# A fused attention and expert kernel: keys and queries transposed and copied one turn earlier, the queries' copy on ScalarE

## The chip, the core and the metric

The kernel runs on one core of a Trainium2 chip. The metric is the time of one execution on the device in microseconds (us). The work lies on five engines that run side by side, each through its own instructions in order: TensorE (PE; its weight loads are shown apart as PEld), VectorE (DVE), ScalarE (ACT), GpSimd (POOL) and SyncE (SP), which here issues the loads from memory.

## What is computed

Three layers in a row, all in 32-bit floats. The change lies in the first.

```python
# q, k, v: 2 batches x 8 heads x 768 positions x 64
k_sum = k.reshape(B, H, nb, 32, D).max(axis=3)      # one key per block of 32
v_sum = v.reshape(B, H, nb, 32, D).mean(axis=3)
scores_l = scale * q @ k.T        # kept where |row - column| < 16
scores_s = scale * q @ k_sum.T + log(32)
a = softmax(concatenate([masked scores_l, scores_s]))
x = a @ concatenate([v, v_sum])
# then: each of the 1536 rows of x goes through one of 8 experts (512 -> 1024 -> 512, relu),
# and all rows through w_in (512 -> 2048), h * cos(h), and w_out (2048 -> 512)
```

## The kernel before

**Pairs and turns.** Attention works on pairs of heads: 8 pairs (2 batches, 4 pairs of heads each), and each pair in two halves of 384 positions, so 16 halves. A loop of 18 turns (L1179) handles them as a pipeline. Half `h` belongs to pair `h // 2`. In turn `i` the engines do, in this order of the code:

- PE transposes the softmax weights of half `i-1` (`attn_turn`, L282, tile `pa`), computes the scores of half `i+1` (`attn_scores`, L247 and L256, tile `ps`) and, when `i` is even, the means of the values of a pair (`prep_v2`, L220, in the same `ps` tile);
- DVE adds the mask to the scores (L264) and takes the negated row maxima (L270, `nmx`); some turns also take the block maxima of the keys (`max_k`, L197, tile `ks`);
- ACT takes the exponentials of half `i` (L275), in even turns copies the values' means out of `ps` (L227, `vsm`), and copies the transposed weights out of `pa` (L290, `aT`);
- PE multiplies the weights of half `i-2` with the values (`attn_av`, L301, tile `po`) and DVE normalizes (L307, L308, L310) into `xb`, the layer's output.

**The keys and queries of a later pair.** They arrive from memory (`load_k`, `load_q`) with positions along the partitions. POOL puts the two heads side by side (`shuffle_k` and `shuffle_q`, L164, tiles `kr` and `qs`, one buffer each, so that a shuffle waits for the transposes that read the one before). PE transposes the result (`turn_heads`, L173) into the PSUM tile `pk` or `pq`, which share one buffer (tag `tr`), and an engine copies that to SBUF as `kT` (`prep_k`) or `qT` (`prep_q`): L186 when ACT does it, L188 when DVE does. There are two sets of `qT`, `kT` and `ks`; pair `n` uses set `n % 2`. At the end of turn `i` (L1242 to L1255) one of these steps is done: for the keys in odd turns, for the queries in even turns, of pair `(i+3)//2`. Pair `n`'s first scores are computed in turn `2n-1`, so its keys are prepared in turn `2n-3` and its queries in turn `2n-2`, the turn just before the scores. `maxima` sends `max_k` of the keys into the next turn (L1212). The names in `ON_VECTOR` (L54) say which copies DVE does; `q2 q4 q6 q8` are the queries' copies at the end of turns 2, 4, 6 and 8. The shuffle of the following pair and the load after that are issued right behind each step.

**What else stands in the turns.** `PLAN` (L47) places the routing to the experts of batch 0 into turns 8 to 13, and the scatter of its rows to memory (`route_scatter`, L536) into turn 13. The expert layer begins after turn 17, with the first 128 scattered rows read back (L745, `xw`), gated on POOL (L758), transposed (L772), copied to `xT` (L774, L775) and multiplied with the weights (L714, first tile `h`). The engines' order inside attention is that of the code (`manual_schedule`); a scheduler orders what follows.

Of the kernel before, what the change touches and what calls it, by code (L numbers as in the profile page):

```python
# [50 lines left out]
)  # L51


ON_VECTOR = "q2 q4 q6 q8 x2 x3 x5"  # L54
NWMAX = 24
TT = 384
TWO_PI = 2.0 * math.pi
# [48 lines left out]
def fused_kernel(ctx, tc, q, k, v, emb, tau, w1, w2, w_in, w_out, consts, out):  # L106
# [36 lines left out]
    def load_vw(b, g, half, vw):  # L143

        h0 = 2 * g
        t0 = 1 - half
        for hh in range(2):
            vs = v[b, h0 + hh]
            srcw = bass.AP(
                vs.tensor, vs.offset + (48 + 64 * (NU - 1) * half) * D,  # L150
                [[D, KW], [64 * D, NU - 1], [1, D]],
            )
            nc.sync.dma_start(vw[0:KW, hh, t0:t0 + NU - 1, 0:D], srcw)
        n = KW - WIN
        if half == 0:
            dst, src = vw[WIN:KW, :, 0, 0:D], v[b, h0:h0 + 2, 0:n]
        else:
            dst, src = vw[0:n, :, NU - 1, 0:D], v[b, h0:h0 + 2, S - n:S]
        nc.sync.dma_start(dst, src.rearrange("h c d -> c h d"))
# [36 lines left out]
    def max_k(bf):  # L196
        nc.vector.tensor_reduce(  # L197
            bf["ks"], bf["kT"][:, WIN:WIN + S].rearrange("d (n r) -> d n r", r=BLK),
            axis=AX.X, op=ALU.max,
        )  # L200
# [24 lines left out]
    def evac_v(pv, ap):  # L225
        vsm = ap.tile([P, 2, D], F32, tag="vsm", name="vsm", bufs=1)
        nc.scalar.activation(vsm[KW:KC], pv, AF.Copy)  # L227
        return vsm
# [8 lines left out]
    def attn_scores(half, bf, ps_s, ap, va=None):  # L237
        qT, kT, ks = bf["qT"], bf["kT"], bf["ks"]


        ps = ps_s.tile([P, 2, 512], F32, tag="s", name="ps")
        for u in range(NU // 2):
            for hh in range(2):
                for m in range(2):
                    t = NU * half + 2 * u + m
                    hp = slice(64 * hh, 64 * hh + 64)
                    nc.tensor.matmul(  # L247
                        ps[64 * m:64 * m + 64, hh, u * KC:u * KC + KW],
                        lhsT=qT[hp, t * 64:(t + 1) * 64], rhs=kT[hp, t * 64:t * 64 + KW],
                        start=True, stop=True,  # L250
                    )
        for u in range(NU // 2):
            for hh in range(2):
                t = NU * half + 2 * u
                hp = slice(64 * hh, 64 * hh + 64)
                nc.tensor.matmul(  # L256
                    ps[:, hh, u * KC + KW:(u + 1) * KC],
                    lhsT=qT[hp, t * 64:(t + 2) * 64], rhs=ks[hp, :], start=True, stop=True,
                )
        pv = ps[KW:KC, 0, 3 * KC:3 * KC + 2 * D].rearrange("p (h d) -> p h d", h=2)  # L260
        if va is not None:
            prep_v2(va, pv)
        s = ap.tile([P, NU, KC], F32, tag="s", name="s")
        nc.vector.tensor_tensor(  # L264
            s.rearrange("p (a u) c -> p a (u c)", a=2), ps[:, :, 0:3 * KC],
            mask[:, 3 * half * KC:3 * (half + 1) * KC].unsqueeze(1).to_broadcast([P, 2, 3 * KC]),
            op=ALU.add,
        )
        nmx = ap.tile([P, NU], F32, tag="nmx", name="nmx")
        nc.vector.tensor_reduce(nmx, s, axis=AX.X, op=ALU.max, negate=True)  # L270
        return s, nmx, pv

    def attn_exp(s, nmx):
        for u in range(NU):
            nc.scalar.activation(s[:, u, :], s[:, u, :], AF.Exp, bias=nmx[:, u:u + 1])  # L275

    on_vector = set(ON_VECTOR.split())

    def attn_turn(s, ps_a):
        pa = ps_a.tile([P, 8 * P], F32, tag="a", name="pa")[:, 0:NU * P]  # L280
        for u in range(NU):
            nc.tensor.transpose(pa[0:KC, u * P:(u + 1) * P], s[:, u, :], ident)  # L282
        return pa

    def attn_aT(pa, ap, i):
        aT = ap.tile([P, NU * P], F32, tag="aT", name="aT")
        if f"a{i}" in on_vector:
            nc.vector.tensor_copy(aT[0:KC], pa[0:KC])
        else:
            nc.scalar.activation(aT[0:KC], pa[0:KC], AF.Copy)  # L290
        return aT
# [694 lines left out]
    with ExitStack() as actx:  # L986
# [50 lines left out]
        NPR = len(pairs)  # L1037
# [16 lines left out]
        def shuffle_k(n):  # L1054

            if n < NPR:
                shuffle(kns[n % 2], krt, nc.gpsimd)
            if n + 2 < NPR:
                load_k(n + 2)
# [7 lines left out]
        def pair_v(n, eng):  # L1067
            if n < NPR:
                prep_v1(vns[n % 2], va, eng)
            if n + 2 < NPR:  # L1070
                load_v(n + 2)
# [95 lines left out]
        def at(i, place):  # L1167
            for piece in plan.get((i, place), ()):
                next(piece, None)
# [9 lines left out]
        for i in range(NH + 2):  # L1179
            p, odd = divmod(i, 2)  # L1180
            if i == 3:
                nc.sync.dma_start(cst[:, P:], consts[:, P:C_VIND])
                next(setup)
                for b, xb in enumerate(xbs):
                    nc.gpsimd.memset(xb[:, :, DM:ROW], 0.0)
                    nc.gpsimd.tensor_copy(
                        xb[:, :, DM:DM + 1],
                        csa[:, C_TOK - C_VIND + b * NU:C_TOK - C_VIND + (b + 1) * NU].unsqueeze(2),
                    )
            if i == 10:  # L1190
                zt = wp.tile([P, 1024], F32, tag="raw", name="zt", bufs=4)[:, 0:ROW]
                nc.gpsimd.memset(zt[:, 0:DM], 0.0)
                nc.gpsimd.memset(zt[:, DM:ROW], 1e6)
                for r0 in (S, NTOK):
                    nc.sync.dma_start(
                        xs[r0:r0 + WT].rearrange("(a p) d -> p a d", p=P),
                        zt.unsqueeze(1).to_broadcast([P, WT // P, ROW]),
                    )
            at(i, "0")
            if 0 < i <= NH:  # L1200
                pa = attn_turn(ss.pop(i - 1), ps_a)
            at(i, "p")
            pv = None
            if i + 1 < NH:
                n, half = divmod(i + 1, 2)
                sums = half and 0 < n < NPR - 1
                ss[i + 1], nmx[i + 1], pv = attn_scores(
                    half, sets[n % 2], ps_s, ap, va if sums else None
                )
                if not sums:  # L1210
                    pv = None
            if maxima is not None:  # L1212
                max_k(maxima)
                maxima = None
            at(i, "s")
            if i < NH:
                attn_exp(ss[i], nmx.pop(i))
            if pv is not None:
                vsm = evac_v(pv, ap)
                pair_v(n + 2, nc.gpsimd)  # L1220
            if 0 < i <= NH:
                aTs[i - 1] = attn_aT(pa, ap, i)
            at(i, "c")
            if i >= 2:
                b, g = pairs[p - 1]
                last_av = attn_av(g, odd, aTs.pop(i - 2), sets[(p - 1) % 2], xbs[b], ps_s, ap)
                if p + 1 < NPR:
                    load_vw(*pairs[p + 1], odd, sets[(p + 1) % 2]["vw"][odd])
                    if odd:
                        prep_v3(sets[(p + 1) % 2], vsm)  # L1230
            at(i, "h")
            if i < 2:
                prep_v3(sets[i], means_v(va))
                pair_v(i + 1, nc.gpsimd)
                load_vw(*pairs[1], i, sets[1]["vw"][i])
            if i == 0:
                prep_k(sets[1], kr, two_banks(), (nc.scalar, nc.vector))
                max_k(sets[1])
                shuffle_k(2)
                prep_q(sets[1], qs, ps_t, nc.scalar)  # L1240
                shuffle_q(2)
            n = (i + 3) // 2  # L1242
            if i and n < NPR:
                if odd:
                    pk = ps_t.tile([P, 8, P], F32, tag="tr", name="pk")
                    prep_k(
                        sets[n % 2], kr, [pk], [nc.vector if f"k{i}" in on_vector else nc.scalar]
                    )
                    maxima = sets[n % 2]
                    shuffle_k(n + 1)  # L1250
                else:
                    prep_q(
                        sets[n % 2], qs, ps_t, nc.vector if f"q{i}" in on_vector else nc.scalar
                    )
                    shuffle_q(n + 1)  # L1255
            at(i, "e")
# [205 lines left out]
```

## Time and profile before

| what | value |
|---|---|
| time, median of 3 runs | 569.94 us (567.6 to 570.23) |
| time of the profiled execution | 571.92 us |
| its span, first to last instruction | 569.9 us |
| mean granted clock of TensorE | 0.959 of full speed |
| PE busy | 526.1 us (92%) |
| DVE busy | 400.1 us (70%) |
| ACT busy | 299.8 us (53%) |
| POOL busy | 94.7 us (17%) |

The profile is of one execution. Its span leaves out what lies before the first and after the last instruction, 2.0 us here. A row of a timeline gives the start from the beginning of the span, the time taken, engine, line, operation, the tile written and the tiles read, shapes and how many instructions are merged; in brackets stands the idle time of the engine just before, and what ended it. The last of several things waited for is named, and at times it is named wrongly. Turn 3 begins on PE at 30.57 us, turn 4 at 35.95, turn 5 at 41.24, turn 7 at 53.48, and turn 9 at 67.35 (there with transposes for the routing).

### The profile page before, as it was taken

Reading aid. Unit: us, or ns where it says so; the run is one execution under the profiler, and the core shown is the slowest. Engines: PE = TensorE matmul, PEld = TensorE weight load, DVE = VectorE, ACT = ScalarE, POOL = GpSimd, SP = SyncE. Lnnn points to the kernel's source line nnn. Section 1 sums busy time; section 2 is a strip of 40 time slices with the busy share of each in tenths; the row PEclk is TensorE's granted clock in tenths of the full one; section 3 lists DMA queues with packets and bytes.
Section 4 is the critical chain, followed back from the end, with each engine's and each line's share of the span. In section 5 each row is a group of like instructions: output and inputs, shape, how many; then the busy total and the mean of one; then the engine's idle time right before and its main releaser. Section 6 shows DMA issues by size and latency. Waiting matters only on the chain. (4 is left out here: it accounts for less than half of the span.)

```text
span 569.9 us, 10621 instructions
## 1 busy us (share of the span) xinstructions
PE 526.1 (92%) x3968; PEld 480.4 (84%) x3968; DVE 400.1 (70%) x830; ACT 299.8 (53%) x637; POOL 94.7 (17%) x116
## 2 busy tenths in 40 slices
PE   6978886759998999999999999999999999999993
PEld 5866765647888999999999998999999999999992
DVE  2476558668677667798977999896579956556662
ACT  2665347758836566575655676643355433333330
POOL 2553323439145110000000000000000000002222
PEclk9798799759999999999999999999999999999998
DMA  8786322778569665767640433322001000001111
GB/s 242 213 229 161 93 96 63 237 275 272 181 212 301 198 217 174 234 200 245 197 136 1 148 114 116 105 74 75 0 1 39 1 1 0 1 0 56 56 57 59
DMA packets 49226, 72.37 MB, mean 127 GB/s; under 512 B 21256, under 2 KB 27656, under 8 KB 49168
## 3 DMA queue, kind: packets, MB, share of 16 engines
q1 hardware_dynamic: 46336, 62.13, 35.9%
q0 software_dynamic: 2832, 9.49, 4.5%
q8 instruction: 33, 0.54, 0.4%
q14 instruction: 25, 0.20, 0.1%
HBM read 64.24 MB, written 7.37 MB: 126 GB/s over the span
## 5 line engine op out<-in xcount | busy, mean ns | idle before, releaser
L714 PE MATMUL po<-sl,gt 128*128 128x512 f32 x567 | 139.3, 390 | 0.0
L714 PEld LDWEIGHTS po<-sl,gt 128*128 128x128 f32 x567 | 105.6, 188 | 17.7
L714 PE MATMUL ph<-yT,sl 128*128 128x384 f32 x576 | 109.6, 339 | 0.0
L714 PEld LDWEIGHTS ph<-yT,sl 128*128 128x128 f32 x576 | 102.8, 188 | 3.8
L624 DVE TENSOR_TENSOR sl<-raw,sl 128x512 fp32r<-128x512 f32 x112 | 73.4, 689 | 17.5 <-ACT sl L623 17.0
L623 ACT ACTIVATE sl<-raw 128x512 fp32r<-128x512 f32 x112 | 64.4, 625 | 22.4 <-PE py L714 12.9
L714 PE MATMUL py<-ht,sl 128*128 128x256 f32 x576 | 72.5, 282 | 0.2 <-DVE ht L810 0.2
L714 PE MATMUL ph<-xT,sl 128*128 128x256 f32 x576 | 71.7, 282 | 0.0
L714 PEld LDWEIGHTS ph<-xT,sl 128*128 128x128 f32 x576 | 69.6, 189 | 0.7 <-issue 0.6
L714 PEld LDWEIGHTS py<-ht,sl 128*128 128x128 f32 x576 | 68.9, 188 | 1.0 <-issue 0.6
L967 POOL DMA_INDIRECT out_dram<-acc,perm x12 | 12.0, 1000 | 344.8 <-DVE acc L1372 342.4
L924 ACT ACTIVATE u<-u 128x384 f32<-128x384 f32 x64 | 33.6, 524 | 62.5 <-DVE u L923 62.4
L928 ACT ACTIVATE gt<-t 128x384 fp32r<-128x384 f32 x63 | 33.1, 525 | 31.3 <-DVE t L927 31.1
L920 ACT ACTIVATE t<-ph 128x384 f32<-128x384 f32 x64 | 31.3, 489 | 33.4 <-PE ph L714 33.0
L927 DVE TENSOR_TENSOR t<-ph,u 128x384 f32<-128x384 f32 (+1 forms) x66 | 35.7, 544 | 17.7 <-ACT u L924 17.4
L929 DVE TENSOR_TENSOR gt<-t,gt 128x384 fp32r<-128x384 f32 x63 | 35.1, 556 | 17.2 <-ACT gt L928 17.2
L922 DVE TENSOR_SCALAR u<-t 128x384 f32<-128x384 f32 x64 | 22.9, 358 | 29.1 <-ACT t L920 27.4
L714 PE MATMUL ph<-yT,early 128*128 128x384 f32 x192 | 36.3, 338 | 0.2 <-DVE yT L1319 0.2
L923 DVE TENSOR_TENSOR u<-t,u 128x384 f32<-128x384 f32 x64 | 35.5, 555 | 1.1
L714 PEld LDWEIGHTS ph<-yT,early 128*128 128x128 f32 x192 | 34.0, 188 | 1.6 <-DVE yT L1319 0.5
L264 DVE TENSOR_TENSOR s<-ps,csa 128x720 f32<-128x720 f32 x16 | 14.5, 907 | 29.4 <-PE ps L256 16.1
L275 ACT ACTIVATE s<-s,nmx 128x120 f32<-128x120 f32 x96 | 29.0, 382 | 8.1 <-DVE nmx L270 6.7
(182 smaller groups left out, 674.2 us busy)
## 6 DMA issues: line engine op xcount, KB each, us to landing
raw<-in_moe_w_dram SPq DMA_DIRECT2D x56, 512.0 KB, 4.5
raw<-in_moe_w_in_dram SPq DMA_DIRECT2D x16, 512.0 KB, 3.7
raw<-in_moe_w_out_dram SPq DMA_DIRECT2D x16, 512.0 KB, 4.3
vw<-in_v_dram SPq DMA_DIRECT2D x32, 120.0 KB, 3.5
xw<-xs POOLq DMA_DIRECT2D x6, 516.0 KB
kn<-in_k_dram SPq DMA_DIRECT2D x8, 384.0 KB, 6.4
qr<-in_q_dram SPq DMA_DIRECT2D x8, 384.0 KB, 4.4
vn<-in_v_dram SPq DMA_DIRECT2D x8, 384.0 KB, 6.8
```

The costliest lines, as they stand in the source:

```text
L264: nc.vector.tensor_tensor(s.rearrange("p (a u) c -> p a (u c)", a=2), ps[:, :, 0:3 * KC], mask[:, 3 * half * KC:3 * (half + 1) * KC].unsqu ...
L275: nc.scalar.activation(s[:, u, :], s[:, u, :], AF.Exp, bias=nmx[:, u:u + 1])
L623: nc.scalar.activation(sl[:, 0, c], r, AF.Copy)
L624: nc.vector.tensor_tensor(sl[:, 1, c], r, sl[:, 0, c].bitcast(F32), op=ALU.subtract)
L714: nc.tensor.matmul(acc, lhsT=lw(a), rhs=lx(c), start=(first and i == 0), stop=(last and i == 2))
L920: nc.scalar.activation(t, ph, AF.Copy, scale=1.0 / TWO_PI, bias=0.25)
L922: nc.vector.tensor_scalar(u, t, ROUND, -ROUND, op0=ALU.add, op1=ALU.add)
L923: nc.vector.tensor_tensor(u, t, u, op=ALU.subtract)
L924: nc.scalar.activation(u, u, AF.Sin, scale=TURN)
L927: nc.vector.tensor_tensor(g, ph[:, cs], u[:, cs], op=ALU.mult)
L928: nc.scalar.activation(gt[:, 0], g, AF.Copy)
L929: lo = nc.vector.tensor_tensor(gt[:, 1], g, gt[:, 0].bitcast(F32), op=ALU.subtract)
```

## The change

The queries leave `ON_VECTOR`, so ACT makes all their copies. The pair that is prepared at the end of turn `i` is now `i // 2 + 2`: its keys in even turns, its queries in odd turns, from turn 0 on. So pair `n`'s keys are prepared in turn `2n-4` and its queries in turn `2n-3`, each one turn earlier than before, and the last step falls in turn 11 and no longer in turn 12.

```diff
-ON_VECTOR = "q2 q4 q6 q8 x2 x3 x5"
+ON_VECTOR = "x2 x3 x5"
...
-            n = (i + 3) // 2
-            if i and n < NPR:
-                if odd:
+            n = i // 2 + 2
+            if n < NPR:
+                if not odd:
                     pk = ps_t.tile([P, 8, P], F32, tag="tr", name="pk")
                     prep_k(
                         sets[n % 2], kr, [pk], [nc.vector if f"k{i}" in on_vector else nc.scalar]
```

The order of PE at the end of turn 0 and in turn 1 (`pk`, `pq`: transposed keys and queries; `pa`: weights; `ps`: scores; `pv`: means of the values), where the first unchanged row is the keys of pair 1:

```order
 L173 MATMUL pk<-cst,kr 128x128 x6
 L173 MATMUL pq<-cst,qs 128x128 x6
+L173 MATMUL pk<-cst,kr 128x128 x6
 L282 MATMUL pa<-cst,s 120x128 x6
 L247 MATMUL ps<-kT_135,qT_134 64x96 x12
 L256 MATMUL ps<-ks_136,qT_134 128x24 x6
 L220 MATMUL pv<-va,csa 24x128 x3
-L173 MATMUL pk<-cst,kr 128x128 x6
+L173 MATMUL pq<-cst,qs 128x128 x6
```

The keys of pair 2 now stand ahead of the first weights' transposes, and the queries of pair 2 take the place that these keys had; from there on keys and queries swap places turn by turn.

ACT from the exponentials of turn 3 to those of turn 5, before:

```order
L275 ACTIVATE s<-s,nmx 128x120 x6
L290 ACTIVATE aT<-pa 120x768
L186 ACTIVATE kT_135<-pk 128x768
L275 ACTIVATE s<-s,nmx 128x120 x6
L227 ACTIVATE vsm<-ps 24x128
L290 ACTIVATE aT<-pa 120x768
L348 ACTIVATE esq,en<-big 8x512
L275 ACTIVATE s<-s,nmx 128x120 x6
```

and with the change:

```order
L275 ACTIVATE s<-s,nmx 128x120 x6
L290 ACTIVATE aT<-pa 120x768
L186 ACTIVATE qT_134<-pq 128x768
L275 ACTIVATE s<-s,nmx 128x120 x6
L227 ACTIVATE vsm<-ps 24x128
L290 ACTIVATE aT<-pa 120x768
L186 ACTIVATE kT_130<-pk 128x768
L348 ACTIVATE esq,en<-big 8x512
L275 ACTIVATE s<-s,nmx 128x120 x6
```

The even turn has a keys' copy where ACT had none, between `aT` and the next exponentials; in the odd turn the copy is that of queries.

DVE at the end of turn 4, in turn 5 (second L264) and up to turn 5's normalizing (`tauc` is a routing constant):

```order
 L310 TENSOR_TENSOR xb_218<-po,rs 128x3x128
-L188 TENSOR_SCALAR qT_134<-pq 128x768
 L350 RECIPROCAL tauc<-tauc 128x1
 L264 TENSOR_TENSOR s<-ps,csa 128x720
 L270 TENSOR_REDUCE nmx<-s 128x6
+L197 TENSOR_REDUCE ks_131<-kT_130 128x24
 L307 TENSOR_SCALAR rs<-po 128x6
 L308 RECIPROCAL rs<-rs 128x6
```

The queries' copy is gone from DVE, and the block maxima of the keys have come from the even turn into the odd one.

## Rows read from the trace of the kernel before

**Rows 1.** Busy time by stretch: PE, PEld, DVE, ACT, POOL (instructions), granted clock, DMA share, GB/s.

```profile
30.57:41.24 10.67, 8.64 (x150) 7.32 (x151) 6.97 (x13) 6.00 (x17) 4.81 (x10) 1.00 0.88 204
41.24:53.48 12.24, 10.54 (x154) 8.97 (x154) 7.88 (x17) 6.60 (x19) 4.57 (x7) 0.86 0.63 174
53.48:67.35 13.87, 11.72 (x151) 10.07 (x151) 7.09 (x14) 5.95 (x16) 4.68 (x6) 0.75 0.39 103
...
126.15:569.90 443.75, 430.00 (x2650) 400.42 (x2650) 328.19 (x674) 233.40 (x470) 47.99 (x43) 0.99 0.35 113
```

**Rows 2.** PE's timeline, turns 0 to 5: start, us, what, idle before.

```profile
20.45 1.48 PE L282 MATMUL pa<-cst,s 128*120 128x128 f32 x6
...
27.44 0.84 PE L220 MATMUL ps<-va,csa 128*24 128x128 f32 x6 [0.42 <-POOL va L213]
...
30.57 0.87 PE L282 MATMUL pa<-cst,s 128*120 128x128 f32 x6 [0.58 <-ACT aT L290]
32.90 0.73 PE L247 MATMUL ps<-kT,qT 64*64 64x96 f32 x24 [1.46 <-DVE qT L188]
...
35.95 0.82 PE L282 MATMUL pa<-cst,s 128*120 128x128 f32 x6
...
41.24 0.87 PE L282 MATMUL pa<-cst,s 128*120 128x128 f32 x6 [0.56 <-ACT aT L290]
43.60 0.72 PE L247 MATMUL ps<-kT,qT 64*64 64x96 f32 x24 [1.48 <-DVE qT L188]
```

**Rows 3.** What PE waited for from 30.57 to 126.2: total us, times, longest.

```profile
PE ps L247 <- DVE qT L188: 4.5, 3, 1.6
...
PE pxa L368 <- DVE xb L310: 1.5, 2, 0.9
```

**Rows 4.** DVE's timeline in turn 4.

```profile
39.08 0.91 DVE L264 TENSOR_TENSOR s<-ps,csa 128x720 f32<-128x720 f32 x1 [1.81 <-PE ps L220]
...
40.84 0.94 DVE L197 TENSOR_REDUCE ks<-kT 128x24 f32<-128x768 f32 x1
...
42.59 0.95 DVE L188 TENSOR_SCALAR qT<-pq 128x768 f32<-128x768 f32 x1
```

**Rows 5.** ACT's timeline, turns 1 to 4.

```profile
24.25 0.27 ACT L227 ACTIVATE vsm<-pv 24x128 f32<-24x128 f32 x1 [0.34 <-PE pv L220]
...
36.15 0.81 ACT L186 ACTIVATE kT<-pk 128x768 f32<-128x768 f32 x1 [3.23 <-PE pk L173]
36.86 1.81 ACT L275 ACTIVATE s<-s,nmx 128x120 f32<-128x120 f32 x6
40.08 0.27 ACT L227 ACTIVATE vsm<-ps 24x128 f32<-24x128 f32 x1 [1.42 <-POOL va L213]
40.38 0.81 ACT L290 ACTIVATE aT<-pa 120x768 f32<-120x768 f32 x1
```

**Rows 6.** POOL's timeline, turns 0 and 3.

```profile
21.05 0.83 POOL L164 TENSOR_SCALAR kr<-kn 128x768 f32<-128x768 f32 x1
...
35.40 0.83 POOL L232 TENSOR_SCALAR vw<-vsm 24x768 f32<-24x768 f32 x1 [2.94 <-DMA vw<-in_v_dram]
```

**Rows 7.** PE's timeline, turns 10 to 13.

```profile
88.19 0.39 PE L437 MATMUL pr<-oh,cst 128*128 128x48 f32 x2 [2.91 <-DVE rs L307]
...
98.49 0.87 PE L282 MATMUL pa<-cst,s 128*120 128x128 f32 x6 [1.19 <-ACT aT L290]
101.10 1.24 PE L247 MATMUL ps<-kT,qT 64*64 64x96 f32 x24 [1.74 <-ACT qT L186]
```

**Rows 8.** DVE's timeline, turns 12 and 13.

```profile
101.18 0.17 DVE L476 TENSOR_SCALAR gate<-gate 128x6 f32<-128x6 f32 x1
103.79 0.91 DVE L264 TENSOR_TENSOR s<-ps,csa 128x720 f32<-128x720 f32 x1 [2.44 <-PE ps L256]
```

**Rows 9.** POOL's timeline: the first of six scatters, turn 13.

```profile
106.69 1.60 POOL L536 DMA_INDIRECT xs<-xb,posi  x1 [0.48 <-DVE big L310]
```

**Rows 10.** PE's timeline: the first matmuls of the expert layer.

```profile
126.15 1.22 PE L714 MATMUL h<-sl,xT 128*128 128x512 f32 x2 [2.92 <-DVE xT L775]
```

## The prediction, made before the changed kernel ran

> **What bounds the kernel now.** I read the busy time by stretch first. From 126.15 us on, the expert layers keep PE at work for 430.0 of 443.75 us at a clock of 0.99, so nothing is to be had there; attention before it has gaps [rows 1]. A pair of turns takes 10.67 us at full clock (30.57 to 41.24, PE busy 8.64), then 12.24 us at 0.86, then 13.87 us at 0.75. If attention ends earlier, the expert layer starts earlier, and PE-bound work behind it moves as a whole.
>
> PE's timeline and its waits show the gaps. In turns 3, 5 and 7 the scores wait for `qT` on DVE: 1.46 and 1.48 us in the rows, 4.5 us for three, so the third took 1.6 [rows 2, 3]. The weights' transposes ahead of them wait 0.58 and 0.56 us for `aT` on ACT [rows 2]. DVE's timeline says why `qT` is late: its copy stands last in a queue of work that begins with the mask at 39.08, has `max_k` at 40.84 (0.94 us), and comes to `qT` at 42.59, ending at 43.54; the scores start at 43.60 [rows 4, 2]. PE had finished the transposes long before.
>
> ACT's timeline shows the other chain. The copy of the means (`vsm`) starts at 40.08, right behind the mask's end at 39.08 + 0.91 = 39.99; the profile names POOL, but both read the same PSUM tile and I read it as a wait for the mask [rows 4, 5]. Then `aT` runs from 40.38 to 41.19, and turn 5 begins on PE at 41.24. This chain holds no query copy, so the change leaves it.
>
> **The change, part by part.** The sum is against the profiled execution, 571.92 us, which lies 2.0 us above the median of the three runs, 569.94; I carry the difference over to the median.
>
> 1. *The start, turns 0 to 2: a loss of 1.9 us.* In turn 0 the keys of pair 2 now go ahead of `pa`, which began at 20.45 [rows 2]. They need POOL's shuffle, which ends at 21.05 + 0.83 = 21.88 [rows 6]. With 0.7 us for the six transposes (turn 3's `pa` group of the same six matmuls, 0.87 with its drain, bounds it from above) `pa` begins at about 22.65, 2.2 us late. ACT has the keys' copy (0.81 us, the row of 36.15) ahead of the exponentials and of `vsm`; `vsm` had 0.34 us of waiting to give, so the lag there is 1.85 us [rows 5]. It goes on through POOL's `va`, for which PE already waited, to the means at 27.44 [rows 2]. Bounds: nothing lost, were the shuffle early, and 2.2 + 1.3 us if PE's clock, still low at 20.45 (1.48 us for six transposes against 0.82 at 35.95), rises later. I take 1.9, from the chain's own rows.
>
> 2. *Turns 3, 5 and 7: 1.46 + 1.48 + 1.6 = 4.5 us gained* [rows 2, 3]. The queries were copied a turn before, so scores start right behind `pa`. Turn 3's part pays back most of the start. What is late next is `aT` in even turns, the 0.56 us that stay; I expect a pair of turns at 10.67 - 1.48 = 9.2 us.
>
> 3. *The copies on ACT: nothing on the path.* DVE loses four of 0.95 us and ACT gains four of 0.81 [rows 4, 5]. In an even turn the new keys' copy follows `aT`, which ends 5.24 us into the turn (41.19 - 35.95), and holds the exponentials behind it: copy to 6.0, exponentials (1.81) to 7.8, next `aT` (0.81) to 8.5, with each row's overlap about 0.1 less [rows 2, 5]. PE asks for these at 9.2, the start of the next even turn, so about 0.7 us is over. The odd turn's copy was there before, for keys. ACT's cover is this 0.7 us; if it goes, 0.81 per pair comes onto the path.
>
> 4. *Shuffles and loads, one turn earlier: nothing.* POOL has 4.81 busy of 10.67 us, and the keys' shuffle and the queries' shuffle only swap turns [rows 1]. SP's loads of keys and queries move ahead of loads of values by up to a turn; the DMA share is 0.88, then 0.63 and 0.39, and the bytes are the same. The nearest row for a bad case is POOL's longest wait for a load in these turns, 2.94 us, which PE did not feel [rows 6]; so 0 to 2.9, and I take 0, since each buffer is asked for a turn or more after its load.
>
> 5. *The clock: 4.7 us gained.* [...] Both falls follow a wait for `qT`. With that wait gone PE has 0.56 us idle in 9.2. Bounds: 0 if the falls stay, 4.7 if both go. I take 4.7, because the stretch would then be busier than the first pair, which kept 1.00; but that first pair had the same waits and no fall, so the wait alone does not decide. [...]
>
> 6. *`max_k` in odd turns: nothing in turns 8 and 9, then a gain.* In turn 8 the routing's transposes wait for `xb` on DVE, and again in turn 9 (1.5 us, two times) [rows 3]. Turn 8 loses a `max_k` of 0.94 ahead of it and turn 9 gains one: about 0. In turn 10 PE waits 2.91 us for DVE's routing (the row names the neighbour) and DVE has one `max_k` less: 0.9 gained. Turn 11 takes it on DVE but not on ACT, so `pa` of turn 13 comes from 98.49 to about 97.6 [rows 7].
>
> 7. *Turn 13: 3.7 us gained in all with item 6.* The queries' copy was ACT's here, and the scores waited for it until 101.10 [rows 7]; now they follow `pa` by 0.75, at 98.3. DVE then sets the pace: its routing chain ended at 101.18 + 0.17 = 101.35 and without turn 12's `max_k` and 0.4 us of earlier start is done at about 100.05; the mask, before at 103.79, goes to 100.1, 3.7 earlier [rows 8]. Two steps on, the gate that the scatter needs comes 3.7 earlier, and so the scatter at 106.69 [rows 9], the rows read back behind it, SP's weight loads queued behind that read, and the first expert matmuls at 126.15 [rows 10]. Bounds: 1.3 (what the table of experts, which starts the first weight loads, gains) to 3.7.
>
> Sum: -1.9 + 4.5 + 4.7 + 3.7 = 11.0 us, that is 571.92 - 11.0 = 560.9 profiled, and **558.9 us** as median.
>
> **The rivals.**
> - *The falls of the clock stay* (0.20): items 1 to 4, 6, 7 as above, without item 5: 569.94 - 6.3 = 563.6. For it: the first pair shows that waits do not decide alone. Against: both falls come right behind one.
> - *The start of the expert layer is set by the weights* (0.08): item 7 gives 1.3 and not 3.7: 561.3. For it: the first weight loads leave when the table is written, on DVE ahead of the mask. Against: the loads that follow wait in SP's queue behind the read of scattered rows.
> - *ACT's queue takes the place of DVE's* (0.04, slower). One mechanism: the keys' copy stands in front of the next exponentials, and when its transposes come over 0.7 us later than in item 3, exponentials, `aT` and the next `pa` wait in a ring. Then no `qT` wait is gained, the start's 1.9 stays, and four copies at 0.71 (0.81 less overlap) are added, with clock and tail as before: 569.94 + 1.9 + 2.8 = 574.6. Against it: ACT is busy 6.0 of 10.67 us [rows 1].
> - *The step is earlier in name only* (0.06): the transposes wait for a shuffle in every turn, as in turn 0, and land where they were: 568 to 570. Against: after turn 0 each shuffle has a turn's time, and POOL is half idle.
>
> **The numbers.** The forecast has 0.62. Its own error is about 2.5 us each way (the runs of before spread over 2.6, and the start may cost 1.6 more). The range goes from 555.5 to 565.5: the lower end is the forecast less the spread and a start that costs less, the upper end the clock rival with 1.9 us of late loads or start. Forecast, clock and weights rivals, 0.90, lie in it but for their tails. A change under 0.5% (2.85 us) can't be told from none: faster 0.90, same 0.06, slower 0.04.
>
> **What would show it.** Right: no wait of the scores for `qT` in turns 3 to 13, a pair of turns near 9.2 us with a 0.5 us wait for `aT`, a clock of 1.00 from turn 2 to turn 9, one PE wait near 20.6 of 1.3 us for POOL's `kr`, the scatter 11 us earlier than 106.69 and the first matmul on `h` near 115. Wrong: `pa` waiting for `aT` by over 1 us in odd turns too (ACT's ring), a clock below 1.00 in those turns (item 5), or an `h` that comes as early as said with the span not following it.

## The result, and the profile after

| | before | after |
|---|---|---|
| time, median of 4 runs each | 569.4 us | 560.96 us |
| the runs | 567.6, 568.86, 569.94, 570.23 | 560.28, 560.42, 561.5, 571.9 |
| profiled execution, its span | 571.92, 569.9 us | 561.5, 559.9 us |
| mean granted clock | 0.959 | 0.964 |

The ratio is 0.9852, 95% interval 0.9817 to 0.9887: the changed kernel is 1.5% faster, and 560.96 lies 2.1 us above the forecast of 558.9, inside its range. The run at 571.9 is left out of the ratio; experiments 1 and 5 to 8 look for the cause of such runs.

Busy time by stretch of the changed kernel, for the pairs of turns 3 and 4, 5 and 6, 7 and 8 (columns as in [rows 1]), and the expert layer:

```profile
32.61:41.75 9.14, 8.58 (x150) 7.33 (x150) 6.12 (x11) 6.69 (x18) 4.81 (x10) 1.00 0.96 223
41.75:51.27 9.52, 9.13 (x154) 7.62 (x155) 7.02 (x15) 7.35 (x20) 4.58 (x7) 1.00 1.00 231
51.27:60.41 9.14, 8.58 (x150) 7.32 (x151) 6.22 (x12) 6.69 (x18) 4.66 (x6) 1.00 0.62 162
118.60:559.90 441.30, 430.45 (x2650) 400.40 (x2650) 328.91 (x675) 233.33 (x470) 46.70 (x42) 0.99 0.35 114
```

The pairs, 10.67, 12.24 and 13.87 us before, are near the 9.2 of the forecast, and the clock is 1.00 in all three. What PE waits for from 20 to 60 us (total, times, longest) has no `qT` left:

```profile
PE pa L282 <- ACT aT L290: 1.5, 4, 0.6
PE pk L173 <- POOL kr L164: 1.3, 1, 1.3
PE ps L220 <- POOL va L213: 0.4, 1, 0.4
```

PE's timeline shows the price at the start, in turn 0, and turn 3:

```profile
17.88 1.49 PE L173 MATMUL pq<-cst,qs 128*128 128x128 f32 x6
20.65 1.54 PE L173 MATMUL pk<-cst,kr 128*128 128x128 f32 x6 [1.28 <-POOL kr L164]
21.98 1.49 PE L282 MATMUL pa<-cst,s 128*120 128x128 f32 x6
...
32.61 0.87 PE L282 MATMUL pa<-cst,s 128*120 128x128 f32 x6 [0.58 <-ACT aT L290]
33.41 0.73 PE L247 MATMUL ps<-kT,qT 64*64 64x96 f32 x24
```

In turns 9 and 10 something new stands on PE, with `max_k` on DVE ahead of it:

```profile
70.00 0.76 PE L368 MATMUL pxa<-cst,xb 128*128 128x128 f32 x5 [1.42 <-DVE xb L310]
72.31 1.54 PE L282 MATMUL pa<-cst,s 128*120 128x128 f32 x6 [1.10 <-ACT big L371]
73.77 1.51 PE L380 MATMUL pl<-big,enT 128*32 128x384 f32 x8
```

```profile
67.95 0.94 DVE L197 TENSOR_REDUCE ks<-kT 128x24 f32<-128x768 f32 x1
69.39 0.56 DVE L310 TENSOR_TENSOR xb<-po,rs 128x384 f32<-128x384 f32 x1
```

The six transposes, 0.87 us at 62.98 at a granted clock of 1.00, take 1.54 there, and the clock from 72.31 to 75.20, the first part of turn 10, is 0.50. Busy time (columns as above) from the first of the routing's transposes to turn 10's `pa`, and in turn 10, first before and then after:

```profile
67.35:79.24 11.89, 8.55 (x107) 6.41 (x107) 7.56 (x15) 4.94 (x12) 3.35 (x6) 1.00 0.37 99
79.24:88.65 9.41, 6.49 (x94) 4.87 (x94) 5.72 (x14) 6.01 (x17) 2.67 (x3) 1.00 0.36 115
```

```profile
60.41:72.31 11.90, 8.55 (x108) 6.43 (x108) 6.75 (x12) 5.59 (x13) 3.35 (x6) 1.00 0.33 95
72.31:81.78 9.47, 8.03 (x93) 5.62 (x94) 4.25 (x13) 4.55 (x12) 1.83 (x2) 0.82 0.26 77
```

Up to turn 10 nothing is lost: the second wait for `xb` is longer (1.42 us, 0.56 before), but the first one, 0.9 us before [rows 3], is gone. In turn 13 the scores follow `pa` directly (before, 1.74 us of waiting, [rows 7]), the mask comes at 94.82 and not at 103.79 [rows 8], and the first scatter and the first matmul on `h` answer to [rows 9, 10]:

```profile
91.62 0.87 PE L282 MATMUL pa<-cst,s 128*120 128x128 f32 x6 [1.84 <-ACT aT L290]
92.42 0.94 PE L247 MATMUL ps<-kT,qT 64*64 64x96 f32 x24
93.30 1.48 PE L256 MATMUL ps<-ks,qT 64*128 64x24 f32 x12
...
118.60 6.68 PE L714 MATMUL h<-sl,xT 128*128 128x512 f32 x18 [3.74 <-DVE xT L775]
```

```profile
97.72 1.23 POOL L536 DMA_INDIRECT xs<-xb,posi  x1 [0.48 <-DVE big L310]
```

**Where the 10.0 us of span come from** (lengths of the stretches between the marks above, before and after):

| stretch | before | after | gained | forecast |
|---|---|---|---|---|
| start to turn 3 | 30.57 | 32.61 | -2.0 | -1.9 |
| turns 3 to 8 | 36.78 | 27.80 | 9.0 | 9.2 |
| turn 9 to the first scatter | 39.34 | 37.31 | 2.0 | 3.7 |
| scatter to first `h` | 19.46 | 20.88 | -1.4 | 0 |
| first `h` to the end | 443.75 | 441.30 | 2.4 | 0 |

The last two nearly cancel. From the first scatter to the end it is 463.2 us before and 462.2 after, and 460.1 to 464.4 in the ten other profiles of the study in which nothing is stuck. To within some 2 us, what attention gains up to that scatter is gained at the end.

What the first matmul on `h` waits for is `xT`, and ACT's timeline shows why that is late. ACT's copy to `xT` stands behind casts of weights (L623), and these wait for memory, first before and then after:

```profile
122.19 1.15 ACT L623 ACTIVATE sl<-raw 128x512 fp32r<-128x512 f32 x2 [4.37 <-DMA raw<-in_moe_w_dram]
```

```profile
114.82 1.15 ACT L623 ACTIVATE sl<-raw 128x512 fp32r<-128x512 f32 x2 [6.81 <-DMA raw<-in_moe_w_dram]
```

In all fourteen profiles of the study the first matmul on `h` begins 3.8 to 4.1 us after this cast. The four weight loads issued ahead of the scatter feed the eight casts before it; this one needs the fifth, which SP issues 0.6 us after the read of the scattered rows (117.72 before, 109.98 after). So the start of the expert layer hangs on the scatter by way of that read and of one weight load behind it. Of the 1.4 us lost there, 1.2 lie between the first scatter and the read (11.0 us before, 12.3 after).

### The profile page after: what moved, and what is told of

It is laid out like the page before. It is cut to its first block, busy times and chain, and to the rows that moved or that the text cites. A ratio compares the mean times of both kernels' runs of the same rounds, so it can differ in the third digit from the quotient of the medians.

```text
span 559.9 us, 10616 instructions
## 1 busy us (share of the span) xinstructions
PE 525.1 (94%) x3968; PEld 478.2 (85%) x3968; DVE 396.6 (71%) x826; ACT 302.2 (54%) x641; POOL 92.9 (17%) x116
## 5 line engine op out<-in xcount | busy, mean ns | idle before, releaser
L623 ACT ACTIVATE sl<-raw 128x512 fp32r<-128x512 f32 x112 | 64.2, 625 | 26.0 <-PE py L714 13.0
L714 PE MATMUL ph<-yT,early 128*128 128x384 f32 x192 | 36.3, 338 | 0.2 <-DVE yT L1319 0.2
L264 DVE TENSOR_TENSOR s<-ps,csa 128x720 f32<-128x720 f32 x16 | 14.5, 907 | 22.3 <-PE ps L256 12.1
```

The costliest lines, as they stand in the source:

```text
L264: nc.vector.tensor_tensor(s.rearrange("p (a u) c -> p a (u c)", a=2), ps[:, :, 0:3 * KC], mask[:, 3 * half * KC:3 * (half + 1) * KC].unsqu ...
L623: nc.scalar.activation(sl[:, 0, c], r, AF.Copy)
L714: nc.tensor.matmul(acc, lhsT=lw(a), rhs=lx(c), start=(first and i == 0), stop=(last and i == 2))
```

## The experiments

Each group was timed beside the kernel before: 569.43 us in the first (1 to 4), 569.86 in the second (5 to 8), 572.58 in the third (9 to 12). Since these differ by 3 us for one and the same kernel, times of different groups are compared by their ratios.

**1. Earlier, but copied on DVE.** In the changed kernel:

```diff
-ON_VECTOR = "x2 x3 x5"
+ON_VECTOR = "q1 q3 q5 q7 x2 x3 x5"
```

> The changed kernel with the queries of pairs 2 to 5 copied on DVE again, so that of the change only 'a turn earlier' is left. Theory (the turn's lead is what removes the wait for qT, and DVE has room for the copy there): within 1 us of the changed kernel, about 561, no wait for qT in turns 3 to 8, clock 1.00 there. Rival (taking the copy from DVE's queue is what does it): the waits for qT or new ones for xb and the mask come back, and the time is near the kernel before, 567 to 570.

Measured: 571.68 us (562.25 to 575.59, 10 runs). By the time alone the rival has won; the profile says otherwise. PE's waits hold no `qT`, a pair of turns has clock 1.00, and the first scatter comes at 95.96, 10.7 earlier than before. The time is lost later, as PE's, DVE's and POOL's timelines show:

```profile
136.26 3.36 PE L714 MATMUL y<-sl,ht 128*128 128x512 f32 x7 [10.28 <-ACT ht L849]
```

```profile
122.65 11.22 DVE L1279 COPY wtc<-wti 3x2 int32<-3x2 int32 x1
```

```profile
121.53 12.33 POOL L1268 MEMSET yT<- 128x1792 f32 x8
```

DVE's copy of six numbers (the table of the first windows) lasts from 122.65 until the last of eight memsets ends on POOL, 121.53 + 12.33 = 133.86; the weights' casts behind it wait. Experiment 4 has the same, 10.02 us. In the changed kernel's own profile that copy stands at 122.56, memsets run from 121.44, and it takes 0.49, ending with the first memset (121.44 + 1.60 = 123.04). It came 1.1 us after the memsets began, as in experiment 1, and took no longer than the 0.15 to 0.53 us of the kernel before and experiments 2 and 3, in which no memset runs beside it. Before, it stood ahead of the copy to `xT`, at 125.1, and the memsets began at 130.73. The change has moved it behind four casts, onto the memsets. Experiments 5 to 8 follow this up.

**2. Copied on ACT, but not earlier.** In the kernel before:

```diff
-ON_VECTOR = "q2 q4 q6 q8 x2 x3 x5"
+ON_VECTOR = "x2 x3 x5"
```

> The kernel before with only the queries' copy moved to ACT, nothing earlier. Theory (DVE's queue made qT late, ACT is free behind aT): the three waits of 1.5 us shrink to 0.5 or less, the clock stays up in turns 3 to 8, nothing is lost at the start and turn 13 stays as before: 569.4 - 4 - 4.7 = about 561. Rival (the lead of a turn is needed): ACT's copy holds the exponentials, qT is as late, 568 to 571.

Measured: 562.83 us, ratio 0.9885 (0.9787 to 0.9983). No wait for `qT` in turns 3 to 8, and the first two pairs are those of the changed kernel:

```profile
28.11:37.24 9.13, 8.57 (x150) 7.31 (x150) 6.09 (x12) 6.68 (x18) 4.79 (x10) 1.00 1.05 242
37.24:46.76 9.52, 9.13 (x155) 7.63 (x155) 6.93 (x16) 7.36 (x20) 4.58 (x7) 1.00 0.85 215
```

So ACT alone is enough there. It keeps the start too (turn 3 at 28.11). What the lead still buys is turn 13: here the scores wait 2.32 us for `qT`, and from `pa` to the scatter it takes 8.8 us where the changed kernel has 6.1. The scatter comes at 99.50, later than the changed kernel's 97.72 although attention led by 4.5 us in turn 3. The larger part of that, 3.3 us, is lost in turns 11 and 12, which take 13.11 us, with a clock of 0.67 from 80 to 90 us, where the changed kernel and the kernel before have 9.84 at 1.00; that the lead prevents this fall isn't shown.

**3. The wait filled with work.** In the kernel before, turns 3, 5 and 7 do the weights' transposes three times over:

```diff
...
-pa = attn_turn(ss.pop(i - 1), ps_a)
+pa = attn_turn(ss.pop(i - 1), ps_a, 3 if i in (3, 5, 7) else 1)
```

> The kernel before with the six transposes of the weights done three times over in turns 3, 5 and 7, so that PE works through most of the 1.5 us in which the scores wait for qT. The wait for qT itself stays. Theory (idle PE in those waits lets the clock fall): clock 1.00 through turns 3 to 8, the pairs 10.7 to 11 us each, and 4 to 5 us off: about 565. Rival (the falls have another cause): clocks of 0.86 and 0.75 stay, about 569 to 571.

Measured: 566.62 us, ratio 0.9948 (0.9905 to 0.999): PE does more and the kernel is faster. The pairs, where before had 1.00, 0.86 and 0.75 [rows 1]:

```profile
28.52:39.20 10.68, 9.96 (x163) 8.64 (x163) 6.98 (x13) 6.12 (x17) 5.30 (x10) 1.00 0.87 210
39.20:49.88 10.68, 10.29 (x166) 8.94 (x166) 7.78 (x17) 6.71 (x19) 4.56 (x7) 1.00 0.73 197
49.88:60.67 10.79, 9.96 (x162) 8.64 (x162) 7.09 (x14) 6.06 (x16) 4.66 (x6) 1.00 0.49 132
```

`qT` is as late as before; only PE isn't idle until it comes (it waits 0.15 to 0.27 us there, 1.46 to 1.6 before). That bears item 5 out: with the idle time in these waits filled, the clock stays at 1.00. More than half of the 4.6 us gained here is lost again: from turn 9 to the scatter it takes 42.2 us, 39.3 before, and the clock there is 0.91 from 60 to 80 us and 0.83 from 80 to 100: the six transposes take 1.54 us at 64.41 and 1.50 at 82.95, where before had 0.87 and 0.83 at the same steps.

**4. The start kept.** In the changed kernel, turn 0 does what it did, and the keys of pair 2 come in turn 1:

```diff
+            if i == 1:
+                prep_k(sets[0], kr, two_banks(), (nc.scalar, nc.vector))
+                maxima = sets[0]
+                shuffle_k(3)
             n = i // 2 + 2
-            if n < NPR:
+            if i and n < NPR:
```

> The changed kernel with turn 0 as it was before: the keys of pair 2 are prepared in turn 1, ahead of its own work on queries, so PE does not wait for POOL's shuffle in turn 0. Theory (the stall in turn 0 is what the change costs at the start, 2 to 3.3 us): the first matmuls of turn 3 come near 30.6 where the changed kernel has 32.6, and the time is 558 to 559. Rival (the start is set by a later chain, POOL's va and the copy of the means): turn 3 begins as in the changed kernel, 561, or the keys' step in turn 1 costs as much there.

Measured: 567.15 us (557.29 to 572.24, 10 runs). Turn 3 begins at 30.92, the scatter comes at 95.18, and the stuck copy hides the rest; no verdict before experiment 8.

**5. The changed kernel again.** No edit.

> The changed kernel itself once more, beside the three that follow, because of what the profiles of the early-on-DVE and the start-kept kernels show: DVE's copy of the window table (3x2 int32, SBUF to SBUF), which the change puts behind four casts of weights, comes at the start of eight POOL memsets and took 11.22 and 10.02 us instead of 0.49, until the last memset ended. Theory (DVE and POOL share something that such a copy needs, and whoever holds it at that moment decides): the executions fall into two groups about 10 us apart, near 560.5 and near 571, the second one in a quarter to three quarters of them. Rival (the late executions come from the chip's state, whatever the kernel): one group, within 2 us, but for single outliers.

Measured: 562.83 us (559.17 to 570.66, 6 runs), ratio 0.9882 (0.9818 to 0.9946): two of six at 569.04 and 570.66, and with the first measurement three of ten. The groups are blurred, 559.2 to 562.9 and 569.0 to 571.9, but no run lies between them. None of the three late runs was traced: that they have the stuck copy is inferred from experiments 1 and 4, whose traced runs have it, and from experiments 6 to 8. A late run alone doesn't show it, since the kernel before, whose copy took 0.44 us in its trace, spreads as widely (564.6 to 583.6 over the three groups).

**6. The same with the copy made in two.**

```diff
-c0 = nc.vector.tensor_copy(wti0[0:3, 0:2], wtis[0][0:3, 0:2])
+for c in range(2):
+    c0 = nc.vector.tensor_copy(wti0[0:3, c:c + 1], wtis[0][0:3, c:c + 1])
...
```

> The changed kernel with that copy of 3x2 numbers made as two copies of 3x1, in the same place of DVE's order. [...] Rival (any DVE copy is held up by POOL, or the late executions have another cause): the group near 571 stays.

Measured: 561.73 us (558.62 to 562.78, 6 runs). DVE's and POOL's timelines in the profile:

```profile
122.37 0.20 DVE L1280 COPY wtc<-wti 3x1 int32<-3x1 int32 x2
```

```profile
120.04 6.20 POOL L1268 MEMSET yT<- 128x1792 f32 x4
```

The copies stand in the midst of the memsets and take 0.13 us each. In this and the five other kernels with two copies, none of 32 runs is above 564.8, so the rival is out.

**7. Experiment 1 with the two copies.**

> The early-on-DVE kernel (queries of pairs 2 to 5 copied on DVE, all else as in the change) with the two 3x1 copies. This repeats the first experiment without its late copy. Theory (the lead of a turn is enough, whichever engine copies): 560 to 562. Rival (the copy off DVE's queue is what does it): 566 to 570 although the late copy is gone.

Measured: 560.53 us, ratio 0.9877 (0.98 to 0.9953). The first pair has 9.14 us and clock 1.00, the next 9.81 and 1.00, no `qT` wait in turns 3 to 8. The rival falls: the lead alone is enough as well.

**8. Experiment 4 with the two copies.**

> The start-kept kernel (turn 0 as before, keys of pair 2 in turn 1) with the two 3x1 copies. Theory (the stall in turn 0 costs 2 to 3 us): 557 to 559 in all executions, 2 to 3 below the changed kernel with the same copies. Rival (what the start gains is waited for later, at the scattered rows or the weights): 560 to 561.

Measured: 558.41 us, ratio 0.9844 (0.9792 to 0.9897), beside 561.73 for experiment 6 in the same group: 3.3 less, but the intervals overlap, and one run, at 562.38, lies outside the 557 to 559 of the theory. PE's timeline of the start, to be read beside the changed kernel's:

```profile
18.80 1.33 PE L173 MATMUL pq<-cst,qs 128*128 128x128 f32 x6
19.97 0.82 PE L282 MATMUL pa<-cst,s 128*120 128x128 f32 x6
...
30.10 0.87 PE L282 MATMUL pa<-cst,s 128*120 128x128 f32 x6 [0.58 <-ACT aT L290]
```

In the two profiles turn 3 begins 2.1 us earlier than in experiment 6 (30.10 and 32.22). Another 1.0 comes from turn 9 to the scatter (36.3 us and 37.3), since turn 10 is at full clock here (7.93 us long; 1.00 from 60 to 80 us), although PE waits 1.42 us for `xb` in turn 9 as in the changed kernel.

**9. `max_k` later.** The changed kernel with the two copies, and:

```diff
-            if maxima is not None:
-                max_k(maxima)
-                maxima = None
             at(i, "s")
...
+            if maxima is not None:
+                max_k(maxima)
+                maxima = None
             at(i, "h")
```

> The changed kernel with the two 3x1 copies and with max_k moved behind the attention's averages of the same turn instead of ahead of them, so that in odd turns DVE reaches xb before max_k. Theory (max_k, which now falls into turn 9, makes the routing's transposes wait 1.4 us for xb, and the clock falls in turn 10 behind that): the wait in turn 9 back to about 0.6, the stretch from turn 9 to 11 at clock 1.00, first scatter 1.5 to 2.4 earlier, 559 to 560.5 beside the 561.7 of the same kernel without it. Rival (the half-clock stretch has another cause or turn 13 waits for DVE anyway): 561 to 562.

Measured: 560.11 us (558.05 to 560.5), ratio 0.9788 (0.9731 to 0.9845). The wait for `xb` is back at 0.56 us, and turn 10 is at full clock (1.00 from 70.99 to 78.92):

```profile
68.68 0.77 PE L368 MATMUL pxa<-cst,xb 128*128 128x128 f32 x5 [0.56 <-DVE xb L310]
70.99 0.87 PE L282 MATMUL pa<-cst,s 128*120 128x128 f32 x6 [1.10 <-ACT big L371]
```

From turn 9 to the scatter it takes 35.9 us (59.95 to 95.81) where the changed kernel took 37.3: 2.4 us are gained up to the end of turn 10 (0.9 of waiting, 1.5 in turn 10), and 1.0 is lost again in turn 13, whose six transposes take 1.54 us at 88.75 (0.87 in the changed kernel). The ratio is lower than in experiment 6, but its interval touches that one's; the theory rests on the trace, and the trace shows only a part of it. The profiles of experiments 1, 4 and 8 have the 1.42 us wait too and a turn 10 of 7.93 us at 1.00. So the fall stands behind the wait in four of the seven profiles that have it, and in none of the three without it (experiments 9 to 11): the wait alone does not make it.

**10. Start kept, two copies, late `max_k`.**

> Start kept, two 3x1 copies and late max_k in one kernel. Theory (the two losses stand in different stretches and add): 1 to 2 us below the 558.4 of the start-kept kernel with the copies, 556.5 to 557.5. Rival (the start-kept kernel has no half-clock stretch in turn 10, so late max_k has only the wait of 0.8 us to give): 557.5 to 558.5.

Measured: 558.19 us (556.59 to 563.23), ratio 0.9776 (0.9722 to 0.983), the lowest ratio of the study; the changed kernel was not timed in this group, and experiment 9, which was, took 1.9 us more. The time lies in the rival's range and not in the theory's, and the trace bears the rival out: experiment 8 has no half-clock stretch in turn 10 that could be removed, and late `max_k` takes the wait for `xb` from 1.42 to 0.56 us. By the ratios, whose intervals overlap, the two can't be told apart. The scatter comes at 92.00, earliest of all.

**11. The same with late loads of the windows' offsets.**

```diff
-            oa = nc.scalar.value_load(wrow(wti, i, 1), min_val=0, max_val=NTOK)
-            ov = nc.vector.value_load(wrow(wti, i, 1), min_val=0, max_val=NTOK)
...
             def y_out(dc, acc):
+                if not at_o:
+                    at_o.append(nc.scalar.value_load(wrow(wti, i, 1), min_val=0, max_val=NTOK))
+                    at_o.append(nc.vector.value_load(wrow(wti, i, 1), min_val=0, max_val=NTOK))
+                oa, ov = at_o
```

> As the one before, with ACT's and DVE's loads of the windows' offsets taken only where the offset is first used, not at the window's head. Theory (in the changed kernel's order that load no longer stands ahead of the next window's copies, so there is nothing left to gain): the same time as the kernel before it within 1 us. Rival (the load still holds ACT somewhere in the expert layer): 1 to 2.5 us less.

Measured: 561.91 us (558.06 to 563.96), neither what the theory nor what the rival said. In its profile 2.6 of the 2.8 us by which the scatter is later than in experiment 10 are there in turn 3 already (31.63 against 29.00), which this edit doesn't touch. No gain can be claimed for it.

**12. Late loads in the kernel before.** The same edit there.

> The kernel before with ACT's and DVE's loads of the windows' offsets taken where the offset is first used. Theory (the 2.40 us in which PE waits for xT in the expert layer at 172.48 come from ACT's load of an offset of the second table, which stands ahead of the copy of xT and waits for that table; in the changed kernel's order it stands behind): that wait goes, and with it 2 to 2.5 us: about 567. Rival (the wait comes from the moment at which the expert layer starts, not from ACT's order): 569 to 570, the wait of 2.4 stays.

Measured: 571.85 us, ratio 1.0001 (0.9964 to 1.0039). The wait is still there, 1.94 us, but the edit did not do what it should: the scheduler put the loads ahead of the copy to `xT` again (the first at 163.5, the copy at 168.91). Against the theory speaks experiment 2, whose order has the loads ahead as well and whose profile has no such wait. Why PE waits for `xT` there in some profiles stays open.

## Why the prediction was right

Time and mechanism were right; one term came out at about half, since it left the clock out, and one effect of the change lay outside what was looked at. By its items:

- **Item 1, the start, was right, and both ends that it gave occur.** PE did wait 1.28 us for POOL's `kr` at 20.65, as foretold. From `pq` in turn 0 to turn 3 it is 11.40 us before (19.17 to 30.57), and 10.4 to 11.9 in all profiles with the old turn 0. Of the six with the new one, four have 13.3 (experiments 1, 5, 6 and 9): 1.9 more than before, the value that was taken. In the changed kernel's own profile the clock was still low at that point (0.50 from 17.88 to 23.40; keys and `pa` take 1.54 and 1.49 us, 0.88 and 0.82 in experiment 5) and it is 14.73, in experiment 7 14.90: 3.3 and 3.5 more, the upper end. The table's 2.0 is less than 3.3, since that execution was 1.29 us ahead at `pq` (17.88 against 19.17). Experiment 8, with 11.30, has lost nothing.
- **Items 2 and 5, turns 3 to 8, were right:** 9.0 us against 4.5 + 4.7. The 4.7 itself no run shows; what the runs showed in its place is the excess of the pairs of 12.24 and 13.87 over that of 10.67, 1.57 + 3.20 = 4.8 us, of which experiment 3 took 4.6. That experiment separates the two items: with the clock kept up (1.00) and `qT` as late as ever, the pairs of 12.24 and 13.87 are back at 10.7 and 10.8. The rival "the falls stay" is out. Experiment 12, with the same attention as before, has its falls in other pairs (12.18, 10.69 and 12.35 us; in the first and the third the keys' six transposes take 1.54 us, in the second 0.88, and the clock from 30 to 60 us is 0.89). So four of six pairs with the idle wait fell, and none of the 36 pairs of the twelve other profiles, in which the wait is gone or filled (9.1 to 10.8 us long). The four fell behind waits of 1.47 to 1.6 us, and the two that did not fall had 1.46 and 1.48 ahead of them. A single wait's length decides nothing here: before, PE waited 2.91 us at 88.19 [rows 7] and ran on at 1.00, while in experiment 2 the same wait of 2.91 us stands ahead of the 13.11 us of turns 11 and 12, with the clock at 0.67 from 80 to 90 us.
- **Items 3 and 4, ACT and POOL at nothing, were right.** PE waits at most 0.6 us for `aT` in turns 3 to 8, and for no load. The rival "ACT's queue" is out. Only in turn 13 does `pa` wait longer for `aT` (1.84 us, 1.19 before [rows 7]); turns 11 and 12 take 9.84 us in both. But neither half of the change was needed for the other: experiments 2 and 7 each reach 9.1 us in the first pair.
- **Items 6 and 7, turns 8 to 13, were too large:** 2.0 us and not 3.7. "Nothing in turns 8 and 9" is right (11.89 and 11.90 us). The step that failed is what follows, which counted DVE's work and left the clock out. The 0.9 us of turn 10 didn't come (9.41 before, 9.47 after), since its first part ran at half clock (0.50); where it didn't, in experiments 8 and 9, turn 10 takes 7.93. In turn 13 the clock falls too, to 0.58 from 92.42 to 94.82, so that the scores and not DVE set the mask's time (it waits 0.5 us for them): 3.2 us from `pa` to the mask, where the item has 2.5, and 2.1 us gained from `pa` to the scatter (8.20 before, 6.10 after) and not 2.8. What makes the clock fall in turn 10 stays open: experiment 9 took the longer wait for `xb` away and the fall was gone, but experiments 1, 4 and 8 have that wait without the fall.
- **The tail** was taken to move as a whole. The sum holds, 463.2 and 462.2 us from scatter to end, though the place of the waits in it changes (-1.4, then +2.4), and the first matmul on `h` came at 118.60 and not near 115. The scatters took longer to land (a median of 6.3 us, 3.5 before). In experiment 2, whose first scatter comes 5.3 us after the first weight load as in the kernel before, it is 3.5 us as well, in experiment 1, with 3.0 us between them (3.3 in the changed kernel), 7.1; that these loads cause it was not tried alone. The +2.4 is as large as the wait for `xT` that experiment 12 is about, but lies within the spread of the ten other profiles, 440.3 to 443.5 us from first `h` to the end.
- **The other rivals.** "Set by the weights" gave 561.3, closer to the 560.96 than the forecast is, but that is luck. The first weight loads, of which it speaks, leave 7.1 us earlier (94.38 after, 101.44 before) and don't hold the start: it is the fifth load that does, and SP has it behind the read of scattered rows, as item 7 says. The end alone couldn't tell the two apart: in the twelve profiles in which nothing is stuck it lies 460.1 to 464.4 us behind the first scatter and 465.4 to 469.5 behind the first weight load. "Earlier in name only" is out, as no shuffle holds PE up after turn 0.
- **Not foreseen:** the copy that the scheduler moved onto the memsets. Three of ten runs of the changed kernel stand about 10 us above the others, and none of the 32 with two copies does. The prediction looked at the order inside attention only.

## What to carry to other kernels

PE's waits for `qT` had two prices here, their own length (4.5 us for three) and the clock behind two of them (0.86 and 0.75 for a pair of turns); both went when work was moved off the late queue (experiment 2) or done earlier (experiment 7), and the second even when PE was given something to do (experiment 3). Look at the clock of the later stretches too: it fell there to 0.67 from 80 to 100 us in experiment 2 and to 0.83 in experiment 3, and 2.9 to 4.3 us were lost again. When an edit changes the time of one part, compare the order of the instructions that a scheduler places in all other parts too, and look at more than one execution: a kernel that is faster in the median may have late runs, here three of ten, about 10 us above the others. If one experiment's time speaks against a theory, read where its time went before dropping the theory.

## What the runs showed of the hardware that was not expected

- A DVE copy of 3x2 numbers within SBUF stood still for 11.22 us beside POOL's memsets of 1.6 us each (experiment 1), while in the changed kernel's profile, begun as far into the first memset, it took 0.49. It doesn't get through at each border between two memsets: in experiment 4 it came at 120.93 and lasted 10.02 us, past the ends of seven of them. As two copies of one number per partition it isn't held at all (0.13 us each in experiments 6, 7 and 8). Both held copies end with the last memset of the row and not with the one that ran when they began (133.87 us against 133.86 in experiment 1, 130.95 against 130.93 in experiment 4). What holds the copy, and why it was not held in the changed kernel's profile, no run shows.
- Three times the transposes in three turns made the kernel before faster, by a ratio of 0.9948 (0.9905 to 0.999).
